# Where a fused attention and gated MLP kernel puts its tokens in order: at the output's stores, or at the exponentials' writes

## The chip, the cores and the metric

The kernel runs on one core of a Trainium2 chip. The metric is the device time of one execution in microseconds (us); lower is better. Engines are named as the profile names them: PE is TensorE (its matmuls; PEld its weight loads), ACT ScalarE, DVE VectorE, POOL GpSimd, and SP SyncE, whose queue issues most of the DMAs. L526 is line 526 of the kernel before.

## What is computed

Attention with normalised queries and keys, whose 12 heads of 64 columns are laid side by side, and behind it an MLP with a spatial gate. With 8 batches, 448 tokens, 768 columns:

```python
q_n, k_n = (rmsnorm(q, g_q), rmsnorm(k, g_k))
scores = scale * np.matmul(q_n, k_n.transpose(0, 1, 3, 2))
scores = scores - np.max(scores, axis=-1, keepdims=True)
attn = np.exp(scores)
attn = attn / (np.sum(attn, axis=-1, keepdims=True) + 1e-09)
attn_out = np.matmul(attn, v)                  # 8 x 12 x 448 x 64
x = attn_out.transpose(0, 2, 1, 3).reshape(8, 448, 768)

h = np.maximum(x @ w_in, 0.0)                  # 768 -> 1024
u, v = h[..., :512], h[..., 512:]
v_n = (v - mu) / np.sqrt(var + 1e-06)          # over the 512 columns
v_s = np.einsum('ts,bsd->btd', w_spatial, v_n) + b_spatial[None, :, None]
out = (u * v_s) @ w_out                        # 8 x 448 x 768, float32
```

## The kernel before

**Order of work.** A text, PLAN, lists some 1,650 operations in the order in which they are issued. `E.0.1/0/a` is operation E with arguments 0 and 1, buffer or PSUM bank 0, on ScalarE (a; v is VectorE, g GpSimd, s SyncE). Every engine runs its own operations in that order and waits by semaphores where it needs a result. SP's queue, too, is one line: loads of q and k (L296), transposes by DMA (L493) and stores (L711, L714) are issued in the plan's order, and one that waits holds up those behind it.

**Token order.** Each of the 448 tokens is numbered 7p + c, with p from 0 to 63 and c from 0 to 6. A load of q, k or v gives a partition p its 7 neighbouring tokens, which are one piece of memory (1792 bytes). After the transposes the tokens of a head pair lie as 7 blocks c of 64 places p. In this order (c, p), block by block, they go through all that follows: the scores' columns, the exponentials, the attention output xt, the MLP, and the output tiles. So an output tile of 128 rows holds two blocks: rows 0 to 63 the tokens 7p + 2m, rows 64 to 127 the tokens 7p + 2m + 1.

**Attention.** Heads go in 24 groups of 4, three for each batch. Operation S makes scores into two PSUM banks by matmuls (L518), keys in the partitions and queries in the columns. E (L526) takes the exponential of both banks into one bf16 tile et of 2 x 448 columns; there are 168 of these on ScalarE and 22 et buffers. Operations s, a and b (L551) multiply et by ones and by v, summing over keys. D and d (L570, L574) make the reciprocal of the sum by a logarithm and an exponential, X (L580) scales the result into xt. The normalisation of q and k ahead of it runs on GpSimd, VectorE and ScalarE (L392 to L438).

**MLP.** V and W (L596, L625) make v in tiles of 128 tokens, with a last tile of 64 (TAIL, tokens from 384); U (L662) makes u with tokens in the columns; H (L676) multiplies by the transposed spatial matrix w_spT; G (L681) gates; O (L690) makes the output tile's two halves of 384 columns, o (L373 on ScalarE, L375 on VectorE) evicts each half from PSUM into one of 5 buffers os, and t stores the tile when both are there. Operation W also makes the 64-row tail of the output of the batch before. Its last occurrence, W.8, makes the last batch's tail alone: half 0 in one bank in partitions 0 to 63, half 1 in another bank in partitions 64 to 127, side by side in the array.

**Spatial matrix.** It is loaded once (64 partitions p, 7 blocks c of 448 columns), transposed by 49 small matmuls (operation Y, L360) and evicted by 4 copies (operation y, L373 and L375). Y picks its 64 columns with a step of 7 from the matrix, so that both axes come out in the order (c, p). The bias row is copied into row 64 of the last tile (operation wx, L375) with the same reordering.

**Stores.** Since a tile's rows are two blocks, each full tile is stored in two DMAs of 64 rows and 192 KB (L714) whose rows lie 7 tokens apart in memory. The tail is one block and one DMA (L711), in the last batch two, one for each half.

Of the kernel before, what the change touches and what calls it, by code (L numbers as in the profile page):

```python
# [11 lines left out]
AF = mybir.ActivationFunctionType  # L12
# [139 lines left out]
o.6.2.1//a u.7.0//a t.6.2 O.6.1.0/2 o.5.0.1//a G.7.3//v H.7.1/1 u.7.2//v t.5.0 o.6.1.0/4/v O.6.1.1/3 H.7.2/5 t.5.2  # L152
o.6.1.1//v H.7.0/4 G.7.2//v t.6.1 G.7.1//v O.6.0.0/7 G.7.0//v O.6.0.1/0 o.6.0.0/2/a O.7.0.0/6 o.6.0.1//a O.7.0.1/2
t.6.0 o.7.0.0/3/a O.7.2.0/3 o.7.0.1//a O.7.2.1/5 t.7.0 o.7.2.0/0/a O.7.1.0/1 o.7.2.1//a O.7.1.1/4 t.7.2 o.7.1.0/1/v
W.8/70 o.7.1.1//a t.7.1 o.7.3.0/4/a o.7.3.1//a t.7.3
"""


# [4 lines left out]
def kernel(  # L163
# [14 lines left out]
    B, H, S, D = q.shape  # L178
# [3 lines left out]
    C = 7  # L182
    T = 64
    TAIL = 384
    scale = 1.0 / math.sqrt(D)
    pe, act, dve, pool, sync = nc.tensor, nc.scalar, nc.vector, nc.gpsimd, nc.sync
    engines = {"a": act, "v": dve, "g": pool, "s": sync}
# [4 lines left out]
    ps = psp.tile([128, 8, 512], FP, name="ps")  # L192

    def several(name, n, shape, dt):
        return [const.tile(shape, dt, name=f"{name}{i}") for i in range(n)]
# [7 lines left out]
    ets = several("et", SLOTS["et"], [128, 2, S], BF)  # L203
# [14 lines left out]
    gts = [gt_all[:, n] for n in range(2)]  # L218
    oss = several("os", SLOTS["os"], [128, DM], FP)
# [7 lines left out]
    w_sp = gt_all.rearrange("p n f s -> p (n f) s")[0:64, 0:C]  # L227
    w_spT = const.tile([128, 4, S], BF, name="w_spT")
# [35 lines left out]
    where = {}  # L264
# [81 lines left out]

    def op_wx(sl, e):
        assert where["wb"]
        copy(engines[e], w_spT[64:65, 3, :].rearrange("q (c p) -> q c p", p=T),
             oss[-1][64:65, 0:S].rearrange("q (p c) -> q c p", c=C))  # L350
        where["wx"] = True

    def op_Y(sl, e, m):

        n = 1 if m == 3 else 2
        where["Y", m] = sl[0]
        p_ = ps[:, sl[0], :].bitcast(BF)
        for a in range(n):
            for c in range(C):
                pe.matmul(out=p_[64 * a:64 * a + 64, T * c:T * c + T],  # L360
                          lhsT=w_sp[:, c, :].rearrange("q (p c) -> q c p", c=C)[:, 2 * m + a, :],
                          rhs=ident[0:64, 0:64], is_transpose=True, start=(c == 0), stop=(c == C - 1),
                          tile_position=(0, 64 * a))

    def op_y(sl, e, m):
        n = 1 if m == 3 else 2
        p_ = ps[:, where.pop(("Y", m)), :].bitcast(BF)[0:64 * n, 0:S]
        copy(engines[e], w_spT[0:64 * n, m, :], p_)
        where["wT", m] = True

    def copy(eng, out, in_):
        if eng is act:
            act.activation(out=out, in_=in_, func=AF.Copy, bias=0.0, scale=1.0)  # L373
        else:
            eng.tensor_copy(out=out, in_=in_)  # L375
# [147 lines left out]
    def op_E(sl, e, G, u):  # L523
        a, b = where.pop(("S", G, u))
        where["et", G, u] = sl[0]
        act.activation(out=ets[sl[0]], in_=ps[:, a:b + 1:b - a, 0:S], func=AF.Exp, bias=0.0, scale=1.0)  # L526

    def et_of(G, r, c):
        if G or c == 6:
# [69 lines left out]
    def tail_at(b, h):  # L599

        return 0 if b == B - 1 and h == 0 else 64

    def op_W(sl, e, b):

        todo = []
        if b < B:
            assert all(where["x", b, j] for j in range(6))
            where["V", b, 3] = sl[0:1]
            passes["V", b, 3] = 3
            for j in range(6):  # L610
                todo.append((j / 6, dict(out=ps[0:64, sl[0], :], lhsT=xts[b % 2][:, j, TAIL:], rhs=w_in[:, j % 2, j // 2, DH:],
                                         start=(j == 0), stop=(j == 5), tile_position=(0, 0))))
        if b > 0:
            assert all(where["g", b - 1, f] for f in range(4))
            for h in range(2):
                where["O", b - 1, 3, h] = [sl[h - 2]]
            for n in range(8):
                h, f = divmod(n, 4)
                at = tail_at(b - 1, h)
                todo.append(((f + 0.5 * h if b == B else n + 0.5) / 8, dict(  # L620
                    out=ps[at:at + 64, sl[h - 2], 0:384], lhsT=gts[(b - 1) % 2][:, f, TAIL:],
                    rhs=w_out[:, f, 384 * h:384 * h + 384], start=(f == 0), stop=(f == 3),
                    tile_position=(0, at))))
        for _, args in sorted(todo, key=lambda x: x[0]):
            pe.matmul(**args)  # L625
# [65 lines left out]
                      rhs=w_out[:, f, 384 * h:384 * h + 384], start=(f == 0), stop=(f == 3))  # L691

    def op_o(sl, e, b, m, h):
        at = 0 if m < 3 else tail_at(b, h)
        rows = slice(at, 128 if m < 3 else at + 64)
        if sl:
            where["os", b, m] = sl[0]
        copy(engines[e], oss[where["os", b, m]][rows, 384 * h:384 * h + 384],
             ps[rows, where.pop(("O", b, m, h))[0], 0:384])
        where["o", b, m, h] = True  # L700

    out_c = [out[b].rearrange("(p c) m -> c p m", c=C) for b in range(B)]

    def op_t(sl, e, b, m):
        t = oss[where["os", b, m]]
        assert where["o", b, m, 0] and where["o", b, m, 1]
        if m == 3:
            for n, at in enumerate(sorted({tail_at(b, 0), tail_at(b, 1)})):
                cols = [h for h in range(2) if tail_at(b, h) == at]
                cols = slice(384 * cols[0], 384 * cols[-1] + 384)  # L710
                engines[(e or "ss")[n]].dma_start(out=out_c[b][6][:, cols], in_=t[at:at + 64, cols])  # L711
            return
        for par in range(2):
            engines[(e or "ss")[par]].dma_start(out=out_c[b][2 * m + par], in_=t[64 * par:64 * par + 64])  # L714

    def op_z(sl, e, n):
        dummies(sl[0], n)
# [5 lines left out]
    for word in PLAN.split():  # L723
        name, sl, e = (word.split("/") + ["", ""])[:3]
# [32 lines left out]
```

## Time and profile before

| | us |
|---|---|
| timed runs | 275.09, 276.58 (median), 278.78 |
| profiled execution | 275.98 |
| its span, first to last instruction | 274.2 |

| engine | where its time goes in the profiled execution |
|---|---|
| PE | scores L518 61.1 us, attention L551 79.9 us in two groups, u L662 43.4, output L690 36.5, v L596 33.9, gate L676 34.8 in two groups |
| ACT | exponentials L526 146.1 us, reciprocals L570 and L574 26.7, evictions L373 16.3, squares L392 14.5 |
| DVE | sums of squares L405 48.5, L580 27.9, L637 21.9, L681 19.2, evictions L375 16.5 |
| POOL | normalisation L438 67.3, squares L394 46.8 |

A group's line has the source line, engine and operation, then output and inputs with their shapes, the count, the busy time in us and the mean in ns of one, and behind the second bar the engine's idle time just before them with what ended it. Busy time of TensorE is that of pipelined matmuls whose ends are modelled, so it says little on how near it is to its peak. A DMA's row on SP is the time that its issue takes on the queue; the transfer lands later (3.2 us in the median for a store of 192 KB). The last issue of a store starts at 270.82 us; the rest of the span waits for landings and closes the program.

### The profile page before, as it was taken

How to read it: one execution, taken by the hardware profiler on the slowest of the kernel's cores; microseconds unless marked ns; L12 is line 12 of the kernel's file. 1: busy time of each engine (PE TensorE's matmuls, PEld its weight loads, DVE VectorE, ACT ScalarE, POOL GpSimd, SP SyncE). 2: the span in 40 equal slices, each digit the busy share in tenths (PEclk: the TensorE clock that was granted, in tenths of full speed). 3: DMA queues.
4: the chain of work that ended last, by engine and by line, in shares of the span. 5: the costliest groups of instructions: out<-in, count | busy, mean ns of one | idle time of the engine just before them, and what ended most of it. 6: DMA issues, size and time to landing. Idle time of an engine off the chain costs nothing.

```text
span 274.2 us, 10148 instructions
## 1 busy us (share of the span) xinstructions
PE 257.9 (94%) x4372; PEld 137.5 (50%) x4389; DVE 203.8 (74%) x355; ACT 217.8 (79%) x357; POOL 145.0 (53%) x122
## 2 busy tenths in 40 slices
PE   7788999999899999999999999989999999999992
PEld 7565564465345455344454454444454545455550
DVE  3788899879859998987985698946976284748730
ACT  4489899999889999988998999988899965330632
POOL 3092994698745898957875669649950000000000
PEclk9959999999999999999999999999999999999998
DMA  7999998999969999999799999976986400114586
GB/s 208 319 344 273 260 171 119 295 204 245 167 145 168 376 177 187 198 251 184 232 184 267 286 246 241 175 95 61 194 114 141 117 2 2 31 29 115 154 279 204
DMA packets 63072, 51.14 MB, mean 187 GB/s; under 512 B 39601, under 2 KB 58674, under 8 KB 63026
## 3 DMA queue, kind: packets, MB, share of 16 engines
q1 hardware_dynamic: 54770, 42.22, 65.4%
q0 software_dynamic: 8256, 8.27, 19.3%
q8 instruction: 34, 0.56, 0.8%
q14 instruction: 12, 0.10, 0.1%
HBM read 38.55 MB, written 11.01 MB: 181 GB/s over the span
## 4 chain that ended last, share of the span: by engine, by line
PE 42%; POOL 13%; DMA 12%; DVE 10%; ACT 10%; issue 10%; SPq 1%; ACTq 0%; POOLq 0%; DVEq 0%
PE ps L551 8%; PE ps L690 7%; POOL nrm L438 7%; PE ps L662 7%; DMA vt<-in_v_dram 6%; ACT et L526 6%; PE ps L676 6%; PE ps L596 5%; PE ps L518 5%; POOL sqt L394 5%; DMA raw<-in_q_dram 3%; DVE ss L405 3%; DMA kr<-nrm 3%; PE ps L625 3%; POOL vt L326 2%
## 5 line engine op out<-in xcount | busy, mean ns | idle before, releaser
L526 ACT ACTIVATE et<-ps 128x896 bf16<-128x896 f32 x168 | 146.1, 923 | 13.4 <-PE ps L518 11.4
L438 POOL TENSOR_TENSOR nrm<-raw,rs 128x896 bf16<-128x896 f32 x40 | 67.3, 1691 | 29.0 <-ACT rs L423 9.4
L518 PE MATMUL ps<-qT,kT 64*32 64x448 bf16 x1344 | 61.1, 357 | 3.2 <-DVE kT L476 1.1
L551 PE MATMUL ps<-et,vt 64*32 64x448 bf16 x1344 | 52.1, 350 | 2.5 <-DMA vt<-in_v_dram 1.0
L394 POOL TENSOR_TENSOR sqt<-raw 128x896 f32<-128x896 f32 x28 | 46.8, 1683 | 13.8 <-DVE vn L653 9.3
L405 DVE TENSOR_REDUCE ss<-sqt 128x14 f32<-128x896 f32 x46 | 48.5, 1076 | 2.9 <-ACT sqt L392 1.2
L662 PE MATMUL ps<-xt,w_in 128*128 128x448 bf16 x192 | 43.4, 353 | 0.2
L518 PEld LDWEIGHTS <-kT 64*32 64x32 bf16 x1344 | 22.2, 90 | 31.7 <-issue 22.5
L690 PE MATMUL ps<-w_out,gt 128*128 128x384 bf16 x192 | 36.5, 326 | 0.1
L580 DVE TENSOR_TENSOR xt<-ps,rc 128x448 bf16<-128x448 f32 x48 | 27.9, 618 | 11.5 <-ACT rc L574 6.9
L596 PE MATMUL ps<-w_in,xt 128*128 128x512 bf16 x127 | 33.9, 380 | 0.9 <-issue 0.3
L551 PEld LDWEIGHTS <-vt 64*32 64x32 bf16 x1344 | 24.9, 92 | 16.2 <-issue 4.2
L373 ACT ACTIVATE os<-ps 128x384 f32<-128x384 f32 (+1 forms) x34 | 16.3, 491 | 15.2 <-PE ps L690 14.6
L551 PE MATMUL ps<-et,ones 64*32 64x448 bf16 x672 | 27.8, 349 | 0.0
L676 PE MATMUL ps<-w_spT,vn 128*128 128x448 bf16 (+1 forms) x128 | 27.7, 353 | 0.2 <-DVE xt L580 0.2
L662 PEld LDWEIGHTS <-w_in 128*128 128x128 bf16 x192 | 17.2, 97 | 20.8 <-issue 7.4
L690 PEld LDWEIGHTS <-gt 128*128 128x128 bf16 x192 | 18.1, 98 | 15.6 <-issue 2.7
L681 DVE TENSOR_TENSOR gt<-ps,us 128x448 bf16<-128x448 f32 x32 | 19.2, 619 | 9.0 <-PE ps L676 5.9
L637 DVE BATCH_NORM_STATS2 s<-vs 128x6 f32<-128x512 bf16 (+1 forms) x32 | 21.9, 683 | 1.6 <-ACT vs L587 1.1
L375 DVE COPY os<-ps 128x384 f32<-128x384 f32 (+1 forms) x30 | 16.5, 555 | 8.9 <-PE ps L690 5.5
L326 POOL DMA_DIRECT2D vt<-in_v_dram x34 | 23.0, 681 | 0.0
L589 DVE TENSOR_SCALAR vs<-ps 128x512 bf16<-128x512 f32 (+1 forms) x24 | 16.3, 683 | 7.4 <-PE ps L596 3.5
(63 smaller groups left out, 253.5 us busy)
## 6 DMA issues: line engine op xcount, KB each, us to landing
out_dram<-os SPq DMA_DIRECT2D x55, 192.0 KB, 3.2
raw<-in_k_dram SPq DMA_DIRECT2D x23, 448.0 KB, 5.9
raw<-in_q_dram SPq DMA_DIRECT2D x23, 448.0 KB, 7.0
vt<-in_v_dram POOLq DMA_DIRECT2D x14, 224.0 KB, 7.3
vt<-in_v_dram POOLq DMA_DIRECT2D x20, 112.0 KB, 5.4
w_in<-in_moe_w_in_dram POOLq DMA_DIRECT2D x8, 192.0 KB, 12.8
w_out<-in_moe_w_out_dram POOLq DMA_DIRECT2D x1, 768.0 KB, 8.2
raw<-in_k_dram SPq DMA_DIRECT2D x2, 224.0 KB, 3.7
```

The lines of the kernel that those rows point to most:

```text
L326: pool.dma_start(out=vts[b % 2][64 * halves[0]:64 * halves[0] + 64 * len(halves), g].rearrange("p r c d -> p r (c d)"), in_=src)
L394: port(eng, eng.tensor_tensor(out=t, in0=x, in1=x, op=ALU.mult))
L405: dve.tensor_reduce(out=sss[G % 3][:, i].rearrange("p r c -> p (r c)"), in_=sqt[where.pop(("sq", G, i))].rearrange("p r (c d) -> p (r c) d ...
L438: port(eng, eng.tensor_tensor(out=nrm[sl[0]].rearrange("p c r d -> p r c d"), in0=raw[where["raw", G, i]].rearrange("p r (c d) -> p r c d" ...
L518: pe.matmul(out=ps[at:at + 32, sl[n], 0:S], lhsT=kT[64 * r:64 * r + 64, c, 64 * hh + 32 * x:64 * hh + 32 * x + 32], rhs=qT[64 * r:64 * r + ...
L526: act.activation(out=ets[sl[0]], in_=ps[:, a:b + 1:b - a, 0:S], func=AF.Exp, bias=0.0, scale=1.0)
L551: pe.matmul(out=ps[32 * l:32 * l + 32, where[kind, G][0], 0:S], lhsT=w, rhs=et_of(G, r, c)[at:at + 64], start=(n == 1), stop=(n == C), til ...
L580: dve.tensor_tensor(out=xts[b % 2][:, 2 * g + half, :], in0=ps[:, where.pop(("ab"[half], G))[0], 0:S], in1=rcs[where["rc", G]], op=ALU.mult)
L596: pe.matmul(out=ps[:, bank, :], lhsT=xts[b % 2][:, j, 128 * m:128 * m + 128], rhs=w_in[:, j % 2, j // 2, DH:], start=(n == 1 and j == 2 * ...
L662: pe.matmul(out=ps[:, bank, 0:S], lhsT=w_in[:, j % 2, j // 2, 128 * f:128 * f + 128], rhs=xts[b % 2][:, j, :], start=(n == 1 and j == 2 * ...
L676: pe.matmul(out=ps[:, sl[0], 0:S], lhsT=vns[b % SLOTS["vn"]][rows, m, 128 * f:128 * f + 128], rhs=w_spT[rows, m, :], start=(m == 0), stop= ...
L690: pe.matmul(out=ps[:, sl[0], 0:384], lhsT=gts[b % 2][:, f, 128 * m:128 * m + 128], rhs=w_out[:, f, 384 * h:384 * h + 384], start=(f == 0), ...
```

## The change

The tokens come into natural order at the exponentials. Each exponential reads its two banks as before, but writes the element of block c and place p to column 7p + c of et, so that 64 neighbouring elements that it reads go to places 7 elements apart. All that follows, xt, the MLP and the output tiles, then has tokens 0, 1, 2 and on. The keys keep their order.

For the spatial matrix, Y now reads 64 neighbouring columns, and the four evictions y write with the step of 7 along the other axis. The copy of the bias row loses its reordering. A full output tile is now 128 neighbouring rows of the output and is stored by one DMA of 384 KB; a tail is 64 neighbouring rows.

In the last operation W.8 both halves of the tail go to one PSUM bank (bank 7), half 0 in partitions 0 to 63 and half 1 in 64 to 127, and one eviction on ScalarE takes all 128 rows. Two DMAs store its halves. No other operation of the plan changes its place.

```diff
-W.8/70 o.7.1.1//a t.7.1 o.7.3.0/4/a o.7.3.1//a t.7.3
+W.8/7 o.7.1.1//a t.7.1 o.7.3.0/4/a t.7.3
...
     def op_wx(sl, e):
-        copy(engines[e], w_spT[64:65, 3, :].rearrange("q (c p) -> q c p", p=T),
-             oss[-1][64:65, 0:S].rearrange("q (p c) -> q c p", c=C))
+        copy(engines[e], w_spT[64:65, 3, :], oss[-1][64:65, 0:S])
...
     def op_Y(sl, e, m):
-                          lhsT=w_sp[:, c, :].rearrange("q (p c) -> q c p", c=C)[:, 2 * m + a, :],
+                          lhsT=w_sp[:, c, 128 * m + 64 * a:128 * m + 64 * a + 64],
...
     def op_y(sl, e, m):
-        copy(engines[e], w_spT[0:64 * n, m, :], p_)
+        copy(engines[e], w_spT[0:64 * n, m, :].rearrange("q (p c) -> q c p", c=C),
+             p_.rearrange("q (c p) -> q c p", c=C))
...
     def op_E(sl, e, G, u):
-        act.activation(out=ets[sl[0]], in_=ps[:, a:b + 1:b - a, 0:S], func=AF.Exp, bias=0.0, scale=1.0)
+        act.activation(out=ets[sl[0]].rearrange("q r (p c) -> q r c p", c=C),
+                       in_=ps[:, a:b + 1:b - a, 0:S].rearrange("q r (c p) -> q r c p", c=C),
+                       func=AF.Exp, bias=0.0, scale=1.0)
...
     def op_W(sl, e, b):
-                where["O", b - 1, 3, h] = [sl[h - 2]]
+                where["O", b - 1, 3, h] = [sl[(h - 2) % len(sl)]]
-                    out=ps[at:at + 64, sl[h - 2], 0:384], lhsT=gts[(b - 1) % 2][:, f, TAIL:],
+                    out=ps[at:at + 64, sl[(h - 2) % len(sl)], 0:384], lhsT=gts[(b - 1) % 2][:, f, TAIL:],
...
     def op_o(sl, e, b, m, h):
+        if (b, m) == (B - 1, 3):
+            bank = where.pop(("O", b, m, 0))[0]
+            where["os", b, m] = sl[0]
+            copy(engines[e], oss[sl[0]][:, 0:384], ps[:, bank, 0:384])
+            return
...
-    out_c = [out[b].rearrange("(p c) m -> c p m", c=C) for b in range(B)]
     def op_t(sl, e, b, m):
+        if (b, m) == (B - 1, 3):
+            for h in range(2):
+                engines[e or "s"].dma_start(out=out[b][TAIL:S, 384 * h:384 * h + 384], in_=t[64 * h:64 * h + 64, 0:384])
+            return
...
-                engines[(e or "ss")[n]].dma_start(out=out_c[b][6][:, cols], in_=t[at:at + 64, cols])
+                engines[(e or "ss")[n]].dma_start(out=out[b][TAIL:S, cols], in_=t[at:at + 64, cols])
             return
-        for par in range(2):
-            engines[(e or "ss")[par]].dma_start(out=out_c[b][2 * m + par], in_=t[64 * par:64 * par + 64])
+        engines[(e or "s")[0]].dma_start(out=out[b][128 * m:128 * m + 128], in_=t)
```

## The prediction

> **What bounds the kernel now.** I read the page's busy shares first, then ScalarE's share of the attention stage, the groups of ScalarE, the rows of reads with a step, and the end on SP's queue. The profiled execution spans 274.2 us and took 275.98 us, so 1.8 us lie around the span; the median of the three timed runs is 276.58 us (275.09 to 278.78), 0.6 us above the execution that I count in.
>
> ```profile
> PE 257.9 (94%) x4372; PEld 137.5 (50%) x4389; DVE 203.8 (74%) x355; ACT 217.8 (79%) x357; POOL 145.0 (53%) x122
> L526 ACT ACTIVATE et<-ps 128x896 bf16<-128x896 f32 x168 | 146.1, 923 | 13.4 <-PE ps L518 11.4
> ```
>
> TensorE leads with 94%. The other row is the exponentials: 168 of them make 146.1 of ScalarE's 217.8 us, and what idle time they have before them is mostly a wait for the scores of L518. In the mean ScalarE has 56 us to spare. But the share over the span hides the stage. The next view cuts the stretch from the first exponential's start (14.4 us) to the last one's end (229.8 us); its columns are length, then busy time of PE, PEld, DVE, ACT and POOL, granted clock, DMA share and GB/s.
>
> ```profile
> 14.40:229.80 215.40, 208.63 (x3839) 107.45 (x3858) 171.79 (x287) 196.91 (x312) 141.30 (x112) 0.99 0.94 194
> ```
>
> There ScalarE is busy for 196.9 of 215.4 us: only 18.5 us are free. TensorE has 6.8 us free. So the stage has two engines near their bound, and an exponential that grows by 18.5/168 = 0.11 us uses up all of ScalarE's spare time. Every longer one is paid nearly in full.
>
> **The change: the exponential's write.** The reading side stays in order (two banks of 448 float32). The writing side goes from 896 neighbouring bf16 elements to 14 runs of 64 elements, each element 7 places, 14 bytes, behind the one before. The number of elements is the same. Per element ScalarE takes 0.83 ns now: (923 - 551)/448, with the 551 ns of the logarithm of L570 that reads 448. No ScalarE instruction in the trace writes with a step, so its price must come from the nearest rows. These are the two reads with a step that the kernel has.
>
> ```profile
> L360 PEld LDWEIGHTS <-gt x14: 174/196/198, 20.1 to 21.1; 64*64 64x64 bf16 x14
> L465 PEld LDWEIGHTS <-nrm x7: 106/110/110, 21.3 to 21.6; 128*64 128x64 bf16 x7
> L375 DVE CAST w_spT<-os 1x448 bf16<-1x448 f32 x1 | 1.0, 971 | 0.0
> L589 DVE TENSOR_SCALAR us<-ps 128x448 bf16<-128x448 f32 x22 | 13.4, 619 | 4.0 <-PE ps L662 3.2 <-ACT et L526 0.7
> ```
>
> The first is TensorE's weight load of the spatial matrix: 64 columns of bf16, each 7 elements behind the last, which is just the step in question. It takes 196 ns (the middle of the three durations) where 64 neighbouring columns, a microsecond later and at the same granted clock of 1.00, take 110: 86 ns, or 1.34 ns a column, more. As a whole rate the strided load is up to (196 - 92)/64 = 1.6 ns a column, with the 92 ns that a load of 32 columns takes (L551) standing for the fixed part. The second is VectorE's cast of the bias row, float32 with a step of 28 bytes: 971 ns against 619 for 448 neighbouring float32, 0.79 ns an element more, so some 1.04 + 0.79 = 1.83 ns (1.04 is (1086 - 619)/448, from VectorE's rows of 896 and 448 elements at L394 and L589). So on two engines a stepped stream runs at 1.3 to 1.8 ns an element, and both are slower than the 0.83 at which ScalarE wants to write. Against carrying them over: both are reads, not writes, and other ports; two strided loads in different column groups also run beside each other, so the memory as a whole is not the limit.
>
> I take the mean of the row with the same step and type, 1.47 ns. An exponential then grows by (1.47 - 0.83) x 896 = 573 ns, to about 1.5 us, and 168 of them by 96.3 us. Of that some 14 us fill the stage's idle time: the 13.4 us in front of the exponentials vanish, since TensorE now has the scores ready long before; the rest is waits for other producers. On the path 82 us remain. The ends: nothing at all (0 ns), and the 1.83 ns of the cast, 896 ns each, 150.5 - 14 = 136 us. Below nothing I exclude, as no element is saved.
>
> The Trainium skill ("Vector Engine (DVE) Microarchitecture Reference", 5.2 Measured stream behaviour on trn2) has a VectorE output that jumps at every element at 1.71 ns a column against 1.05; it speaks against this change. The trace's cast agrees in kind, and no run here shows ScalarE; carried over as an estimate, it would make 0.66 x 896 x 168 = 99 us, 3 us more than the sum above.
>
> **The transposed spatial matrix.** The 49 weight loads of L360 become unstepped: up to 49 x 86 ns = 4.2 us less load time, which overlaps in part, so 2 to 3 us of TensorE in the first 22 us. It was waiting there for others anyway (4.8 us idle in the first 26), so I take 0 and keep 2.3 us as the gain's end. The four evictions get the stepped write: 4 x 448 x 0.64 ns = 1.1 us over two engines, once; their readers come first at 63.5 us. The bias copy loses its step: 0.35 us of VectorE at 40 us, nothing on the path.
>
> **The stores.** 24 full tiles take one issue instead of two: 24 x 0.59 us (L714's median) = 14 us of SP's queue. A double-sized issue costs no more: the 448 KB loads of L296 take 0.48 to 0.58 us each. SP spent 68 us waiting for the normalised rows of POOL, which covers all of this before the last tiles; transposes and loads behind a store are issued 0.6 us earlier. No store waits for more than before: each half already waited for both evictions. Buffer os comes free when one 384 KB store has landed instead of two of 192 KB (3.2 us); five buffers rotate, and if that cover went, an eviction would start about a microsecond late.
>
> **The last tail.** Times are start and length in us.
>
> ```profile
> 268.90 0.99 ACT L373 ACTIVATE os<-ps 64x384 f32<-64x384 f32 x2 [0.28 <-PE ps L625]
> 268.91 1.17 SPq L714 DMA_DIRECT2D out_dram<-os  x2
> 270.18 1.18 SPq L711 DMA_DIRECT2D out_dram<-os  x2
> ```
>
> Two evictions of 0.49 us become one of 128 rows, 0.49 us. It must wait for both halves of the product, but already the first one started after the last matmul (268.87), so nothing is lost, and nothing is queued behind it on ScalarE. The two tail stores were held up by SP, which was still issuing the second half of the tile before (to 270.1). Now that tile is issued by 269.5, the eviction ends at 269.4, its store goes 0.28 us later (the same delay as before the store at 268.91), so at 269.7, and the second at 270.25 instead of 270.82: 0.56 us gained on the path, as the last landing follows its issue by 2.2 us as before. If the larger store in front delays that landing, the gain is gone.
>
> Sum: 274.2 + 82 - 0.6 = 355.6 us of span, 357 us with the 1.8 around it.
>
> **The rivals.** First, the write with a step is free, and the forecast falls on the other side. The mechanism: ScalarE writes 2 bytes per 0.83 ns, and its own port can take one separate place in that time, which neither row above measures. It decides from 0.11 us per exponential: below that the idle time pays. Then only the tail is left, 275.98 - 0.6 = 275.4 us, down to 273.1 if the loads of L360 count in full. For it speaks that the two stepped rows are of engines whose reads feed a different pipeline, and that TensorE's loads are paced far faster than ScalarE anyway (98 ns for 128 neighbouring columns, 92 for 32); against it that the row with the identical step is slowed. The Trainium skill ("SBUF — State Buffer", Door 1) says that one can stride for free by up to 8 bf16 elements, and a step of 7 would fall under it; the trace's load at L360 does not agree. Chance 0.38.
>
> Second, only part of the penalty shows, since a write need not be answered: half of it, 0.32 ns an element, makes 48 - 14 = 34 us, so 309 us. Chance 0.05. Third, a write of 2 bytes at a new place costs as much as the cast's element: 275.98 + 136 - 0.6 = 411 us. Chance 0.07. Fourth, the freed SP queue brings transposes and loads forward so far that the stage itself shortens: it would take 5.5 us out of TensorE's 16.3 idle us, of which few waits were for a load or a store. Chance 0.02, some 270 us.
>
> **How the numbers follow.** The forecast has 0.48. Its own range comes from 1.34 and 1.6 ns an element: (0.51 or 0.77) x 896 x 168 = 77 or 116 us, less 14 and 0.6, so 338 to 377 us. The range to hold 8 in 10 must take in the free case too: from 274 to 380 us it holds the forecast, the second rival and most of the first, and leaves out the third, the fourth and the lowest part of the first. About 2%, 5.5 us, is what a measurement of this kernel can tell from no change: faster 0.02 (the fourth), within 0.38 (the first), slower 0.60 (the rest).
>
> **What would show it.** The exponentials' mean: about 1.5 us confirms the main step, 0.92 the first rival, 1.8 the third. ScalarE should be busy nearly without a gap from 14 us to the last exponential, near 312 us, with the waits for L518 gone and TensorE's share down to some 73%. The loads of L360 should fall to about 110 ns, the stores of full tiles to 24 issues near 0.6 us, and the last tail should show one eviction with its store 0.3 us behind. The forecast is wrong if the mean of L526 stays below 1.03 us, or if the path leaves ScalarE: TensorE, idle for short stretches, could be granted a lower clock and become slow itself.

## The result, and the profile after

The changed kernel takes 713.14 us in the median of 6 runs (712.28 to 713.71) against 275.83 us before (274.29 to 278.78): 2.588 times as long, with a 95% interval of 2.579 to 2.597. That is the side that was forecast, and nearly twice the forecast time. The profiled execution spans 711.1 us.

The page of the changed kernel, first the busy shares, then its two costliest groups:

```profile
PE 406.5 (57%) x4372; PEld 168.8 (24%) x4389; DVE 209.7 (29%) x355; ACT 660.3 (93%) x356; POOL 145.2 (20%) x122
L526 ACT ACTIVATE et<-ps 128x896 bf16<-128x896 f32 x168 | 594.6, 3839 | 5.5 <-PE ps L518 5.2
L518 PE MATMUL ps<-qT,kT 64*32 64x448 bf16 x1344 | 98.5, 487 | 205.7 <-ACT et L526 175.0
```

An exponential takes 3839 ns where it took 923. ScalarE has TensorE's place as the bound, and the wait has turned round: before, exponentials waited for scores; now the matmuls of L518 wait 175 us for a bank that an exponential still reads. The chain of work that ended last, by engine and by line, says the same:

```profile
ACT 75%; issue 12%; PE 10%; DMA 1%; DVE 1%; SPq 0%; ACTq 0%; DVEq 0%
ACT et L526 69%; PE ps L692 2%; PE ps L553 2%; PE ps L664 2%; PE ps L678 2%; ACT sqt L392 1%; DMA raw<-in_q_dram 1%; PE ps L518 1%; ACT rc L576 1%; ACT rc L572 1%; PE ps L598 1%; ACT os L373 1%; ACT rs L423 1%; ACT vs L589 0%; ACT ls L418 0%
```

The stretch from the first exponential's start to the last one's end, with the columns of the prediction's view:

```profile
14.70:665.50 650.80, 356.40 (x3844) 138.51 (x3859) 178.49 (x289) 640.00 (x313) 141.57 (x112) 0.64 0.29 64
```

And seven exponentials in a row from ScalarE's timeline (start, length, in us):

```profile
37.01 24.69 ACT L526 ACTIVATE et<-ps 128x896 bf16<-128x896 f32 x7
```

The stage grew from 215.4 to 650.8 us, by 435.4: ScalarE's busy time by 443.1 (196.9 to 640.0), its idle time fell by 7.7 (18.5 to 10.8). What lies outside the stage grew by 1.5 us. So all but 1.5 us of the loss lies in this stage, in the exponentials and what queues with them on ScalarE. The row of seven shows their pace: (24.69 - 3.93)/6 = 3.46 us from one start to the next, with 3.93 us the mean of an exponential behind another one. Over all 102 that start before the record of the exponential in front of them has ended, the median pace is 3.47 us; in the kernel before it is 0.80 us. The difference, 2.67 us, times 168 is 449 us.

TensorE's busy time rose by 149 us, but this bounds nothing: it waits in pieces of up to 3.2 us, and its granted clock falls to 0.64 in the stage.

### The profile page after: what moved, and what is told of

It is laid out like the page before. It is cut to its first block, busy times and chain, and to the rows that moved or that the text cites. A ratio compares the mean times of both kernels' runs of the same rounds, so it can differ in the third digit from the quotient of the medians.

```text
span 711.1 us, 10112 instructions
## 1 busy us (share of the span) xinstructions
PE 406.5 (57%) x4372; PEld 168.8 (24%) x4389; DVE 209.7 (29%) x355; ACT 660.3 (93%) x356; POOL 145.2 (20%) x122
## 4 chain that ended last, share of the span: by engine, by line
ACT 75%; issue 12%; PE 10%; DMA 1%; DVE 1%; SPq 0%; ACTq 0%; DVEq 0%
ACT et L526 69%; PE ps L692 2%; PE ps L553 2%; PE ps L664 2%; PE ps L678 2%; ACT sqt L392 1%; DMA raw<-in_q_dram 1%; PE ps L518 1%; ACT rc L576 1%; ACT rc L572 1%; PE ps L598 1%; ACT os L373 1%; ACT rs L423 1%; ACT vs L589 0%; ACT ls L418 0%
## 5 line engine op out<-in xcount | busy, mean ns | idle before, releaser
L526 ACT ACTIVATE et<-ps 128x896 bf16<-128x896 f32 x168 | 594.6, 3839 | 5.5 <-PE ps L518 5.2
L518 PE MATMUL ps<-qT,kT 64*32 64x448 bf16 x1344 | 98.5, 487 | 205.7 <-ACT et L526 175.0
L518 PEld LDWEIGHTS <-kT 64*32 64x32 bf16 x1344 | 30.0, 99 | 284.0 <-issue 279.4
L553 PE MATMUL ps<-et,vt 64*32 64x448 bf16 x1344 | 80.1, 467 | 14.3 <-ACT et L526 9.7
L664 PE MATMUL ps<-xt,w_in 128*128 128x448 bf16 x192 | 63.6, 476 | 12.7 <-ACT et L526 11.2
L553 PE MATMUL ps<-et,ones 64*32 64x448 bf16 x672 | 49.7, 554 | 15.1 <-ACT et L526 7.7
L692 PE MATMUL ps<-w_out,gt 128*128 128x384 bf16 x192 | 46.6, 387 | 9.4 <-ACT et L526 7.4
L598 PE MATMUL ps<-w_in,xt 128*128 128x512 bf16 x127 | 46.8, 493 | 6.9 <-ACT et L526 3.5
L678 PE MATMUL ps<-w_spT,vn 128*128 128x448 bf16 (+1 forms) x128 | 41.4, 476 | 9.5 <-ACT et L526 9.3
L591 DVE TENSOR_SCALAR us<-ps 128x448 bf16<-128x448 f32 x22 | 13.5, 620 | 50.6 <-PE ps L664 50.4
L553 PEld LDWEIGHTS <-ones 64*32 64x32 bf16 x672 | 18.1, 129 | 33.1 <-issue 32.4
```

What stands on the lines that cost most here:

```text
L518: pe.matmul(out=ps[at:at + 32, sl[n], 0:S], lhsT=kT[64 * r:64 * r + 64, c, 64 * hh + 32 * x:64 * hh + 32 * x + 32], rhs=qT[64 * r:64 * r + ...
L526: act.activation(out=ets[sl[0]].rearrange("q r (p c) -> q r c p", c=C), in_=ps[:, a:b + 1:b - a, 0:S].rearrange("q r (c p) -> q r c p", c= ...
L553: pe.matmul(out=ps[32 * l:32 * l + 32, where[kind, G][0], 0:S], lhsT=w, rhs=et_of(G, r, c)[at:at + 64], start=(n == 1), stop=(n == C), til ...
L591: dve.tensor_relu(out=out, in_=in_)
L598: pe.matmul(out=ps[:, bank, :], lhsT=xts[b % 2][:, j, 128 * m:128 * m + 128], rhs=w_in[:, j % 2, j // 2, DH:], start=(n == 1 and j == 2 * ...
L664: pe.matmul(out=ps[:, bank, 0:S], lhsT=w_in[:, j % 2, j // 2, 128 * f:128 * f + 128], rhs=xts[b % 2][:, j, :], start=(n == 1 and j == 2 * ...
```

## The experiments

The question is why a write with a step of 14 bytes costs 3.3 ns more per element, when the two stepped reads of the kernel before cost about 1 ns more. The theories are in the expectations.

**The step on the read instead.**

```diff
-        act.activation(out=ets[sl[0]].rearrange("q r (p c) -> q r c p", c=C),
-                       in_=ps[:, a:b + 1:b - a, 0:S].rearrange("q r (c p) -> q r c p", c=C),
+        act.activation(out=ets[sl[0]].rearrange("q r (p c) -> q r p c", c=C),
+                       in_=ps[:, a:b + 1:b - a, 0:S].rearrange("q r (c p) -> q r p c", c=C),
...
-        copy(engines[e], w_spT[0:64 * n, m, :].rearrange("q (p c) -> q c p", c=C),
-             p_.rearrange("q (c p) -> q c p", c=C))
+        copy(engines[e], w_spT[0:64 * n, m, :].rearrange("q (p c) -> q p c", c=C),
+             p_.rearrange("q (c p) -> q p c", c=C))
```

> Same tokens in natural order, but every exponential now writes 896 neighbouring elements and takes the step of 64 float32 (256 bytes) on its read from PSUM; the four copies of the spatial matrix likewise. Theory S (a stepped write is what is slow, since an element of 2 bytes at a place of its own is written alone): the exponentials come back to 0.92 us and the kernel to 273 to 277 us. Rival R (any stepped stream of ScalarE is slow, reading or writing): the exponentials stay above 1.5 us and the kernel above 340 us.

Measured: 0.9987 times the kernel before, interval 0.9947 to 1.0026. Its group of exponentials:

```profile
L526 ACT ACTIVATE et<-ps 128x896 bf16<-128x896 f32 x168 | 145.9, 923 | 12.4 <-PE ps L518 10.9 <-PE ps L553 0.7
```

The same 923 ns as before, to the nanosecond. The same elements are moved to the same places, only in another order of time. So neither the permutation nor its PSUM read costs the exponential anything; the write's step alone does. On VectorE the two spatial copies, bf16 out of PSUM, did pay for the step on their read: 620 ns against 387. This version has the change's token order and stores at the time of the kernel before.

**The copies alone, when all is quiet.** Behind the last eviction of the kernel before, 19 copies on ScalarE and 5 on VectorE were appended, three times over. `go(out, in_)` is one copy on ScalarE, `src(0)` two PSUM banks of 448 float32, and `to(t, c)` the same with a write into t that goes on by c elements each time. The main forms are

```python
go(ets[n], src(0))                       # neighbouring
go(*to(ets[n], 7))                       # step of 7; also 2, 4, 8, 16, 64
go(*to(raw[n], 7))                       # the same into float32; also 2, 64
go(ets[n][:, 0].rearrange("q (p c t) -> q c p t", c=7, t=2), ...)   # pairs, 28 bytes apart
dve.tensor_copy(out=ets[n + 4][:, 0], in_=ps[:, 0, 0:S])
dve.tensor_copy(out=ets[n + 4][:, 0].rearrange("q (p c) -> q c p", c=7), ...)   # stepped write, bf16
dve.tensor_copy(out=ets[n + 4][:, 0].rearrange("q (p c) -> q p c", c=7), ...)   # stepped read of PSUM
dve.tensor_copy(out=raw[n + 4][:, 0].rearrange("q (p c) -> q c p", c=7), ...)   # stepped write, float32
dve.tensor_copy(out=ets[n + 4][:, 1].rearrange("q (c p) -> q c p", c=7), ...)   # stepped read of SBUF, float32
```

> The kernel before, with copies appended behind its last eviction, when the other engines are idle; they write scratch and cost the end of the span some 150 us. ScalarE and VectorE copies out of PSUM or SBUF with steps of 1, 2, 4, 7, 8, 16 and 64 elements, of 2 or 4 bytes, single or in runs of 2 or 4. Theory S1 (each lone element of 2 bytes costs a fixed 4.1 ns whatever the step, as bytes of a word must be read before they are written): 3.8 us at every step from 2 on, about 1 us for float32 at any step, and for runs of 2 bf16 elements near the plain 0.55 us. Theory S2 (a place in another line of 16 bytes than the last one costs): 3.8 us from a step of 8 on, clearly less at 2 and 4 bf16 elements, and float32 with a step of 7 as slow as bf16. Theory C (the 3.8 us come from contention with the other engines): near 1.5 us for the step of 7 here, when all is quiet.

ScalarE's durations, each the middle of three that agree within 10 ns; only the plain row took 917 ns once and 896 twice. For the rate per element 170 ns are taken off, which is 917 - 896 x 0.833. The last column is that rate times the number of elements that fall into 16 bytes, so the price of one line of 16 bytes.

| ScalarE out of PSUM, 896 elements | ns | ns per element | ns per line of 16 bytes |
|---|---|---|---|
| bf16, neighbouring | 896 to 917 | 0.83 | |
| bf16, every 4 bytes | 1162 | 1.11 | 4 x 1.11 = 4.4 |
| bf16, every 8 bytes | 2146 | 2.21 | 2 x 2.21 = 4.4 |
| bf16, every 14 bytes | 3626 | 3.86 | 8/7 x 3.86 = 4.4 |
| bf16, every 16 bytes | 4119 | 4.41 | 4.4 |
| bf16, every 32 and 128 bytes | 3905, 4151 | 4.17, 4.44 | 4.2, 4.4 |
| float32, every 8 bytes | 957 | 0.88 | 2 x 0.88 = 1.8 |
| float32, every 28 and 256 bytes | 1767, 1677 | 1.78, 1.68 | 1.8, 1.7 |
| bf16 pairs, 28 bytes apart (448 elements) | 569 | as 448 neighbouring ones: 570 | |
| bf16, neighbouring; PSUM read every 28 or 256 bytes | 917 | 0.83 | |

VectorE's five copies, 448 elements each, as groups of the trace, costliest first (busy us, mean ns). Their lines follow the code above: L758 is neighbouring, L759 the stepped bf16 write, L760 the stepped read of PSUM, L761 the stepped float32 write, L762 the stepped read of SBUF.

```profile
L759 DVE CAST et<-ps 128x448 bf16<-128x448 f32 x3 | 5.7, 1894 | 0.1
...
L762 DVE CAST et<-raw 128x448 bf16<-128x448 f32 x3 | 2.8, 949 | 0.1
L761 DVE COPY raw<-ps 128x448 f32<-128x448 f32 x3 | 2.8, 946 | 0.0
...
L760 DVE CAST et<-ps 128x448 bf16<-128x448 f32 x3 | 1.9, 624 | 0.1
L758 DVE CAST et<-ps 128x448 bf16<-128x448 f32 x3 | 1.9, 617 | 93.5 <-ACT et L735 93.5
```

Neighbouring float32 elements cost no more than neighbouring bf16 ones: the second set of quiet copies, further down, has 544 ns for 448 of them, against 570 here. The copy of 896 of them in this set took 1245 ns, but it begins 0.50 us before the record of the copy in front of it, the one with a step of 128 bytes, has ended (start and length):

```profile
284.33 4.15 ACT L735 ACTIVATE et<-ps 128x896 bf16<-128x896 f32 x1
287.98 1.25 ACT L735 ACTIVATE raw<-ps 128x896 f32<-128x896 f32 x1
```

Contention (C) is out: alone, the step of 14 bytes costs nearly as much as in the kernel. S1 is out as it was put, since the price follows the step up to 16 bytes. S2 has the right unit, but put the same price on 2 and 4 bytes: the last column is constant at about 4.4 ns for lone bf16 elements and at 1.8 for float32. So what ScalarE pays for is a line of 16 bytes, and a line in which lone elements of 2 bytes are written costs 2.5 times as much as one written in words of 4 bytes. Two neighbouring bf16 elements make a word, and their write is free of the penalty even though the pairs are 28 bytes apart. A neighbouring write would not show it, as 8 elements take ScalarE 6.7 ns anyway (8 x 0.833). VectorE, tried with one step for each type, fits the same prices: 1894 ns for lone bf16 elements and 946 for float32, against 617 for neighbouring ones. Reading float32 from PSUM every 256 bytes cost it next to nothing (624).

The reads out of SBUF show what the prediction's rows had measured. ScalarE reading float32 every 28 bytes took 1002 ns against 576, reading bf16 every 14 bytes 892; with 203 ns of fixed part (576 - 448 x 0.833) that is 1.78 and 1.54 ns an element, the second being 7/8 of the first. So ScalarE's read out of SBUF has the price of a line written in whole words.

**Everything but the order.** Exponentials and spatial copies write as in the kernel before, all else is the change:

```diff
-        act.activation(out=ets[sl[0]].rearrange("q r (p c) -> q r c p", c=C),
-                       in_=ps[:, a:b + 1:b - a, 0:S].rearrange("q r (c p) -> q r c p", c=C),
-                       func=AF.Exp, bias=0.0, scale=1.0)
+        act.activation(out=ets[sl[0]], in_=ps[:, a:b + 1:b - a, 0:S], func=AF.Exp, bias=0.0, scale=1.0)
...
-        copy(engines[e], w_spT[0:64 * n, m, :].rearrange("q (p c) -> q c p", c=C),
-             p_.rearrange("q (c p) -> q c p", c=C))
+        copy(engines[e], w_spT[0:64 * n, m, :], p_)
```

> The changed kernel with the exponentials and the four copies of the spatial matrix writing neighbouring elements as before, so the reordering of the tokens is left out and the output's rows stand in another order than the reference's. It shows what the single stores and the single eviction of the last tail are worth alone. Theory S: 275.3 us, that is 0.6 us below before (the first rival of the prediction). Rival: the single stores add something, and the kernel stays above 280 us.

Measured: 0.9978, interval 0.9945 to 1.0011, so 0.6 us less with a margin of 0.9. The stores and the tail are worth what was expected or nothing; this run does not tell which. They cost 0.3 us at most.

**The order made at xt.** Exponentials write as before; VectorE's product reads with the step, and the spatial copies as in the first experiment:

```diff
-        dve.tensor_tensor(out=xts[b % 2][:, 2 * g + half, :], in0=ps[:, where.pop(("ab"[half], G))[0], 0:S],
-                          in1=rcs[where["rc", G]], op=ALU.mult)
+        dve.tensor_tensor(out=xts[b % 2][:, 2 * g + half, :].rearrange("q (p c) -> q p c", c=C),
+                          in0=ps[:, where.pop(("ab"[half], G))[0], 0:S].rearrange("q (c p) -> q p c", c=C),
+                          in1=rcs[where["rc", G]].rearrange("q (c p) -> q p c", c=C), op=ALU.mult)
```

> Natural order, but made where VectorE scales the attention output: 48 products that read PSUM and the reciprocals with a step of 256 bytes and write neighbouring elements; the exponentials write neighbouring elements as before. Theory S (only stepped writes are dear): the products stay at 0.62 us, the kernel at 273 to 277 us. Rival R (stepped reads are dear too): the products go to 1 us or more, 48 x 0.4 us = 19 us of VectorE, of which its idle time in the stage (43 us) hides most: 276 to 285 us.

Measured: 1.0265, interval 1.0215 to 1.0315. Its products, in the kernel before and here:

```profile
L580 DVE TENSOR_TENSOR xt<-ps,rc 128x448 bf16<-128x448 f32 x48 | 27.9, 618 | 11.5 <-ACT rc L574 6.9 <-PE ps L551 3.6 <-PE ps L518 0.9
L580 DVE TENSOR_TENSOR xt<-ps,rc 128x448 bf16<-128x448 f32 x48 | 43.0, 932 | 10.6 <-ACT rc L574 6.2 <-PE ps L551 2.9 <-PE ps L518 1.2
```

The rival is nearly right: 314 ns more each, 15 us of VectorE, of which some 7 us reach the end. The one stepped operand that lies in SBUF is the reciprocal row, read every 256 bytes; at 1.78 ns an element 448 of them instead of VectorE's 1.04 would add 0.33 us, about what is seen. That PSUM's part was free here too is inferred from the copy at L760.

**Pairs with the step, in the kernel.**

```diff
-        act.activation(out=ets[sl[0]].rearrange("q r (p c) -> q r c p", c=C),
-                       in_=ps[:, a:b + 1:b - a, 0:S].rearrange("q r (c p) -> q r c p", c=C),
-                       func=AF.Exp, bias=0.0, scale=1.0)
+        act.activation(out=ets[sl[0]].rearrange("q r s -> q (r s)").rearrange("q (p c t) -> q c p t", c=C, t=2),
+                       in_=ps[:, a:b + 1:b - a, 0:S], func=AF.Exp, bias=0.0, scale=1.0)
```

> The changed kernel, but the exponentials write pairs of neighbouring bf16 elements, and the pairs stand 28 bytes apart (the natural order is left out, and values come to other columns). Theory W (a line of 16 bytes costs a write port 1.78 ns, and 4.4 ns if less than a word of 4 bytes is written in it): 448 lines x 1.78 = 0.80 us plus the fixed part, so the exponentials take 0.92 to 1.0 us and the kernel 275 to 285 us. Rival (the distance is what costs, whatever is written there): two places of 4.4 ns less than before halved, about 2 us each, and the kernel above 420 us.

**A step of 2, in the kernel.** The same place with `c=2` for `c=C`. In this run and the one of the pairs the spatial copies write neighbouring elements.

> The changed kernel, but the exponentials write with a step of 2 elements (4 bytes) instead of 7; natural order is left out. Theory W: four lone elements share a line of 4.4 ns, so 1.1 ns an element and 0.245 us more per exponential, as in the quiet copies (1162 against 917 ns); 168 of them are 41 us, of which 8 to 18 us of ScalarE's idle time in the stage are taken: 299 to 310 us. Rival (the step of 7 was slow by distance beyond 8 bytes or so, as the skill's free steps would have it): 275 to 280 us.

Measured: pairs 1.0164, interval 1.0099 to 1.0229 (280.28 us); the step of 2 elements 1.0819, interval 1.0764 to 1.0875 (298.61 us). The exponentials' group in the kernel with pairs:

```profile
L525 ACT ACTIVATE et<-ps 128x896 bf16<-128x896 f32 x168 | 157.1, 1007 | 8.9 <-PE ps L517 7.5 <-PE ps L551 0.7
```

and in the kernel with the step of 2:

```profile
L525 ACT ACTIVATE et<-ps 128x896 bf16<-128x896 f32 x168 | 185.3, 1214 | 4.2 <-PE ps L517 3.7
```

Writing words 28 bytes apart costs 84 ns more than a plain exponential; writing half words 14 bytes apart costs 2916 more. So distance is not the price. The pairs' exponentials come out just above their forecast of 0.92 to 1.0 us, and the kernel with the step of 2 just under its own. That kernel's stage, in the columns of the prediction's view:

```profile
14.90:253.50 238.60, 221.41 (x3859) 107.49 (x3858) 173.11 (x287) 230.47 (x313) 141.41 (x112) 0.98 0.82 174
```

The median pace of its exponentials from start to start is 1019 ns against 798, so 37 us for 168; ScalarE's busy time in the stage rose by 33.5 us, 10.4 us were taken from the idle time, and the stage grew by 23.2. The way from an exponential's price to the kernel's time, as the prediction took it, holds here too.

**The tail alone**, on the kernel before, with the old token order in the store:

```diff
-W.8/70 o.7.1.1//a t.7.1 o.7.3.0/4/a o.7.3.1//a t.7.3
+W.8/7 o.7.1.1//a t.7.1 o.7.3.0/4/a t.7.3
...
+        if (b, m) == (B - 1, 3):
+            bank = where.pop(("O", b, m, 0))[0]
+            where["os", b, m] = sl[0]
+            copy(engines[e], oss[sl[0]][:, 0:384], ps[:, bank, 0:384])
+            return
```

> The kernel before with only the last tail changed: one bank, one eviction of 128 rows, stored in the old token order, so the result is the same. Prediction's step: the second tail store is issued some 0.3 to 0.5 us earlier, since the two stores of the tile before still fill SP's queue; 276.5 us, no measurable change. Rival: two products in one bank hinder each other, and the last eviction starts later than 0.03 us after the last matmul.

Measured: 1.0021, interval 0.9986 to 1.0056, no difference. In the trace the last eviction starts 0.04 us after the last matmul, so two products in one bank do not hinder each other, but the second tail store is issued 1.89 us after that matmul instead of 1.95, 0.06 us earlier where 0.3 to 0.5 were expected: the eviction saved was not what the store waited for. In the first experiment, where the tile before has one store, it is issued 1.08 us after it.

**More quiet copies.** On the kernel before, among others. Here `flat(n, f)` is 434 elements of et in a row that begin at element f, and `seen(2)` reads as many neighbouring float32 from PSUM:

```python
go(flat(n, 0).rearrange("q (p c t) -> q c p t", c=7, t=2), seen(2))   # pairs from an even element
go(flat(n, 1).rearrange("q (p c t) -> q c p t", c=7, t=2), seen(2))   # pairs from an odd element
act.activation(out=ets[n], in_=ps[:, 0:2, 0:S], func=AF.Exp, bias=0.0, scale=0.0)
act.activation(out=ets[n].rearrange("q r (p c) -> q r c p", c=7), ...)
```

> The kernel before with more quiet copies and exponentials appended behind its end (scratch only; they add some 50 us). Theory W: pairs of bf16 that begin at an even element cost as a plain row (0.57 us for 434 elements), pairs that begin at an odd one cut two words each and cost 1.1 to 1.3 us; float32 with a step of 16 bytes costs 448 x 1.78 + 170 = 0.97 us; an exponential with the step of 7 takes 3.63 us here like the copy, so its further 0.2 us in the changed kernel is the write of the one before that still drains. Rival (pairs are cheap because two elements fall in a line, not because they make a word): odd pairs cost like even ones.

Measured, 434 elements: neighbouring 528 ns, neighbouring from an odd element 534, even pairs 557, odd pairs 1352; float32 every 16 bytes (448 elements) 949. An odd pair cuts two words, and in one of four cases it lies in two lines: 217 pairs x 1.25 lines x 4.4 ns = 1.19 us, and (1352 - 170) ns are 1.18. So it is the word that counts, not that two elements fall in one line. The exponential alone, plain and with the step of 7 (smallest, middle and largest duration in ns):

```profile
L746 ACT ACTIVATE et<-ps x3: 912/912/912, 279.5 to 304.0; 128x896 bf16<-128x896 f32 x3
L747 ACT ACTIVATE et<-ps x3: 3626/3626/3626, 280.4 to 304.9; 128x896 bf16<-128x896 f32 x3
```

In the changed kernel an exponential takes 3.93 us in the mean where it begins before the record of another one has ended (102 of the 168), and the rest take 3.70 (median 3.66), near this one. The 102 begin 0.45 us (median) before that end, so the same time stands in two records. The pace tells more: 784 lines (7/8 of 896) x 4.4 ns = 3.45 us, against 3.47 us measured from start to start.

## Why the prediction was right in kind and wrong in size

- **The bound, right.** ScalarE had 18.5 us to spare in the stage, and the exponentials used them up and went on the path. With the measured pace the prediction's own sum is 168 x 2.67 - 14 = 435 us on the path, and 274.2 + 435 - 0.6 + 1.8 = 710 us; 713 were measured.
- **The step that failed: the price of a stepped write.** "I take the mean of the row with the same step and type, 1.47 ns." That row is a read, and as a read it was well sized: ScalarE reads bf16 with that step at 1.54 ns an element. A write of 2 bytes costs 3.86, so an exponential grew by 2.92 us and not by the 0.573 of the sum. The prediction named the weakness ("both are reads, not writes, and other ports") and still took the row as nearest; its upper end, the 1.83 ns of the cast, was a price of 4-byte elements and no bound for 2-byte ones. The range ended at 380 us for that reason. No row of the kernel before showed a stepped write of 2 bytes on any engine.
- **The page against the change.** The 1.71 ns of the Trainium skill ("Vector Engine (DVE) Microarchitecture Reference", 5.2 Measured stream behaviour on trn2) are for words of 4 bytes. VectorE's stepped float32 copy agrees: 946 - 617 ns over 448 elements are 0.73 ns more than 1.04, so 1.78. Applied to bf16 the figure misses the same factor as the row did.
- **The rivals.** That the step is free (0.38) is refuted by the table; the statement of the Trainium skill ("SBUF — State Buffer", Door 1) that one can stride for free by up to 8 bf16 elements holds here neither for a write by 7 (3.86 ns against 0.83), nor for one by 2 (1.11), nor for a read out of SBUF (1.54). The second, half the penalty, is refuted by the same table. The third rival priced a write above the row taken, and was still far off at 411 us. The fourth, a stage that the freed queue shortens, does not show where everything but the order is changed (0.9978).
- **The idle time, somewhat off.** 14 us of it were to vanish, and 7.7 did: 5.5 of the 13.4 us of waits in front of the exponentials stayed.
- **The spatial matrix, right.** The weight loads lost their step: in the window at full clock they take 110 ns (196 before).

```profile
L359 PEld LDWEIGHTS <-gt x14: 102/110/110, 11.2 to 11.5; 64*64 64x64 bf16 x14
```

- Its four evictions were priced at 1.1 us more in all and cost 6.3 us (two of 2.17 on ScalarE, two of 1.88 on VectorE, against 0.53 and 0.39): the same wrong price. The bias copy did not gain 0.35 us, it lost 0.53; the last section has its wait.
- **Stores and tail, right in size.** The issue of a merged store has a median of 0.36 us (0.59 for a half before). The end of the changed kernel's SP queue, start and length:

```profile
702.04 4.23 SPq L722 DMA_DIRECT2D out_dram<-os  x4
706.72 1.11 SPq L713 DMA_DIRECT2D out_dram<-os  x2
```

- The second tail store goes out 1.08 us after the last matmul and not 1.95, 0.87 us earlier (0.57 were forecast), and the span ends 4.92 us after that matmul instead of 5.33, 0.41 us earlier. The tail alone moved that store by 0.06 us only, so the gain is the freed queue's, as the prediction argued.

## What to carry to other kernels

When a permutation has to be made in a copy or an activation that reads float32 from PSUM, put the step on the PSUM read and write neighbouring elements; if SBUF must be written with a step, keep pairs of bf16 elements together on a word's boundary. A price carried over from another operation has to match it in direction and in bytes per element; a read is no bound for a write. Before forecasting an edit to an instruction that runs 168 times, measure one such instruction at the end of the kernel, where it disturbs nothing.

## What the runs showed of the hardware that was not expected

- A write of ScalarE into SBUF takes about 1.8 ns for each line of 16 bytes that it enters with whole words of 4 bytes (float32 every 8 and 28 bytes: 957 and 1767 ns for 896 elements), and about 4.4 ns where it writes less than a word in it (bf16 every 4 to 128 bytes: 1162 to 4151 ns). VectorE fits at the one step tried for each type (946 ns for 448 float32 every 28 bytes, 1894 for 448 bf16 every 14). Why a part of a word costs more is not shown. The Trainium skill ("SBUF — State Buffer", Specifications (TRN2)) has lines of 16 bytes and a penalty for each crossing; the trace agrees in the unit.
- Reading float32 from PSUM with a step cost ScalarE nothing at 28 and 256 bytes (917 ns) and VectorE next to nothing at 256 bytes (624 against 617). VectorE's bf16 copies from PSUM were not spared: 620 ns with the step, 387 without it.
- The bias cast took 971 ns with its step and 1500 without it, because without it the cast waited for GpSimd. In the kernel before, the cast is done while GpSimd's product still runs; in the changed one it ends 0.25 us behind the product's end (first GpSimd and VectorE before, then after; start and length):

```profile
40.09 1.68 POOL L438 TENSOR_TENSOR nrm<-raw,rs 128x896 bf16<-128x896 f32 x1
40.62 0.97 DVE L375 CAST w_spT<-os 1x448 bf16<-1x448 f32 x1
88.44 1.69 POOL L438 TENSOR_TENSOR nrm<-raw,rs 128x896 bf16<-128x896 f32 x1 [12.06 <-ACT rs L423]
88.88 1.50 DVE L375 CAST w_spT<-os 1x448 bf16<-1x448 f32 x1
```

- All ten traces agree: in the four whose cast has the step it takes 967 to 978 ns beside a running product, in the six without the step it takes 1393 to 1737 ns and ends 0.25 to 0.26 us behind the product. The Trainium skill ("SBUF — State Buffer", Who interferes with whom) has a VectorE cast in a two-port mode share a port pair with GpSimd, so that the second of the two waits for the whole of the first; that would fit. That the step keeps the cast out of such a mode is not shown here.
